# A new list of orders for block-sparse attention and an MLP on one core of a Trainium2

## The chip, the cores and the metric

The kernel runs on one core of one Trainium2 chip. Its engines work beside each other, each through its own instructions in order: PE (matrix products; PEld is its loading of weights), DVE, ACT and POOL (elementwise work), and SP, which here issues DMAs. The metric is the time of one execution on the device in microseconds (us), as the median of several. All operands of the large matrix products are 16-bit floats; sums are kept in 32 bits.

## The reference, cut to what matters

The inputs are q, k and v of shape (4, 8, 768, 64): batch, heads, positions, head dimension. Positions form 12 blocks of 64. Each position takes the 3 blocks with the highest gate score among those that are not later than its own, and its own block; it attends causally inside them. The result goes through a two-layer MLP with the tanh form of gelu.

```python
k_rep = k.reshape(B, H, 12, 64, D).mean(axis=3)
gate_scores = where(causal_block, einsum('bhsd,bhnd->bhsn', q, k_rep), -1e9)
top_idx = argsort(gate_scores, axis=-1)[..., -3:]
mask = (block in top_idx or own block) & (key position <= query position)
attn = softmax(where(mask, (q @ k.T) / 8, -1e9))
x = (attn @ v).transpose(0, 2, 1, 3).reshape(3072, 512)
out = gelu_tanh(x @ moe_w_in) @ moe_w_out          # 512 -> 2048 -> 512
```

## The kernel before, in words

**Tiling.** Heads are taken in pairs: pair p holds heads 2(p mod 4) and 2(p mod 4) + 1 of batch p // 4, so pairs 0 to 15. For each pair q, k and v are loaded, turned so that the head dimension lies on the partitions, and the block sums of k are formed. A gate product gives the block scores, DVE selects the top three, and the selection becomes a mask that is added to the scores. The scores are computed transposed, exponentiated by ACT, their diagonal edges are zeroed by POOL, and they are multiplied with v, which has a column of ones so that the row sums come with the product. The normed result is turned once more into xT. When four pairs of a batch are done, its 768 tokens go through the MLP: the first layer in 16 tiles of 128 hidden channels for two halves of 384 tokens (s1), the second per tile of 128 tokens (s2). In the last three batches some products are formed by seven half-size ones out of sums and differences on DVE (s1_seven, w_sums, half, join); this isn't touched.

**Buffers.** PSUM holds two wide buffers (scores and s1) and four banks, which pre, pv, ops, the tail and the fillers share by fixed numbers. Exponentials have six buffers (ats), the results two (osb, each for a pair of token tiles, so a new tile waits for the stores of the pair before the last), raw v two (vsd); k, q, v and the mask sets have four.

**What sets the order.** The kernel first adds 1962 numbered operations to a plan, each with the engines that can do it, and then emits them by three written lists: ORDER gives the sequence, and with it the order on each engine and in each queue; ENGINE sends some copies to ACT or POOL that else go to the first engine that the operation names (mostly DVE); BUFFER gives, in the order in which buffers are taken, which one. Waits between engines follow from the data and the buffers and are put in by the framework. An engine takes its instructions strictly in order, so one that waits holds all behind it.

```python
for n in ORDER:
    op = self.ops[n]
    for kind, key in op.takes:
        if key not in self.buf:
            self.buf[key] = self.kinds[kind][0][next(picks)]
    op.emit(engine.get(n, next(iter(op.engines))))
```

**Names and lines that the steps touch.** Loads: L387 (q, k, v as they lie), L393 (the ones that DVE turns), L421 (the first pair), cast of v to 16 bits in cast_v (L432, copies at L356 on ACT, L358 on POOL, L360 on DVE). The weights: load_w, a small copy (L451) that orders them behind the loads of v and two DMAs for each matrix issued by POOL (L453). Constants on POOL: the gates' constants (op 0, L480 to L484), the matrix e16 (op 1, a memset L491 and two affine selects L494), and four sets of memsets (ops 2, 3, 4, 5; L502 to L507). Pre, for each pair: transposes (L541) and, for k with block sums, L538; copies; the gate (L680) after the block sums (L582, L588); its turn to rows (L696); the selection sel_e: add the causal constant (L703), MAX8 (L712), compare (L713), and the mask value (L717); mask transposes on PE (L749) or by DMA (L756). Attention of batch 0 (heads2): scores L856, exponentials L875, edges on POOL L901, product with v L924, norm L942 and L943, turn L981. The others (heads): L1039, L1052, L1066, L1078. MLP: s1 L1115 with gelu L1127, s1_seven L1204, s2_plain L1315 with copies to osb and stores L1340, s2 L1365, L1414, L1449. The fillers are small products on zeros (L1517), numbered 1890 and up.

The single operations that the text speaks of: 62 and 71, the first half of k and of q of pair 0 turned on PE; 72 the copy of that q half; 73 and 74 the same for the second half of q; 75 the first gate and 77 its selection, 78 the second gate and 80 its selection; 105 the cast of q of pair 1 on POOL; 94, 114 and 130 copies of k; 30 the cast of v of pair 0 and 198 the first product with v; 139 and 141 the copies of q of pair 3, 142 its gate, 147 the copy of its mask; 227 a copy of turned results, 259 a norm; 363 the first s1 product; 157 and 163 the loads of w_in and w_out, 61 the cast of v of pair 3; 433 the first s2 product; 450, 468, 487, 505 the stores of token tiles 0, 1, 2, 3 of batch 0; 523 and 541 the copies to osb of tiles 4 and 5; 791 and 815 gelus of batch 1, 1044 a cast of q.

Of the kernel before, what the change touches and what calls it, by code (L numbers as in the profile page):

```python
# [21 lines left out]
    5, 2, 1890, 6, 1891, 1892, 1893, 9, 15, 0, 1894, 1895, 1896, 1897, 12,  # L22
    1898, 1899, 1900, 22, 1901, 1902, 1903, 23, 1904, 1905, 1906, 71, 72,
    62, 73, 195, 64, 63, 82, 75, 76, 66, 1907, 3, 77, 1908, 74, 1, 18, 1909,
    67, 1910, 100, 1911, 84, 68, 98, 85, 19, 35, 78, 4, 36, 83, 79, 80, 194,
    200, 99, 31, 89, 91, 101, 93, 86, 90, 120, 95, 87, 94, 196, 201, 121,
    32, 102, 219, 214, 202, 105, 220, 113, 103, 118, 215, 119, 1912, 26,
    109, 205, 104, 27, 197, 44, 115, 48, 106, 210, 107, 30, 198, 45, 111,
    110, 203, 221, 206, 234, 211, 122, 249, 207, 224, 123, 39, 208, 125,
    216, 235, 124, 133, 1913, 250, 240, 40, 229, 114, 251, 134, 212, 129,  # L30
    236, 126, 217, 135, 241, 222, 49, 43, 52, 245, 230, 225, 254, 242, 127,
    1914, 255, 238, 243, 138, 53, 140, 263, 246, 56, 57, 283, 58, 131, 247,
    130, 141, 1915, 1916, 139, 1917, 264, 252, 142, 231, 157, 284, 268, 279,
    256, 145, 232, 285, 143, 265, 269, 270, 1918, 226, 280, 274, 1919, 275,
    163, 144, 146, 276, 237, 61, 155, 227, 147, 288, 153, 1920, 259, 289,
    266, 297, 298, 302, 258, 271, 1921, 292, 272, 1922, 260, 299, 303, 1923,
    277, 149, 308, 322, 151, 323, 281, 286, 304, 169, 290, 293, 300, 309,
    305, 313, 317, 314, 310, 306, 170, 326, 261, 311, 294, 318, 328, 363,
    364, 295, 356, 315, 329, 365, 366, 358, 359, 319, 360, 361, 320, 324,
    327, 367, 362, 352, 353, 354, 355, 330, 171, 408, 174, 175, 357, 178,  # L40
    409, 410, 331, 411, 179, 412, 373, 374, 375, 376, 388, 389, 390, 391,
    377, 392, 403, 404, 405, 433, 393, 406, 434, 394, 395, 182, 396, 407,
    418, 419, 335, 420, 421, 397, 368, 369, 422, 370, 435, 398, 371, 399,
    436, 400, 372, 401, 383, 402, 384, 437, 385, 438, 439, 440, 441, 386,
    387, 336, 442, 443, 428, 429, 430, 444, 337, 183, 423, 186, 431, 424,
    432, 425, 339, 445, 341, 446, 447, 378, 448, 426, 379, 449, 427, 451,
    452, 453, 380, 187, 381, 345, 454, 631, 342, 343, 344, 334, 413, 414,
    632, 584, 692, 415, 346, 585, 455, 456, 457, 416, 458, 338, 635, 586,
    459, 417, 460, 461, 462, 636, 588, 347, 382, 463, 349, 553, 464, 465,
    466, 470, 348, 471, 574, 472, 570, 473, 474, 475, 571, 590, 476, 961,  # L50
    477, 572, 587, 575, 190, 478, 594, 479, 480, 481, 591, 482, 592, 483,
    593, 467, 566, 561, 484, 485, 644, 567, 488, 489, 552, 693, 596, 490,
    598, 491, 595, 562, 492, 493, 568, 557, 494, 569, 554, 647, 495, 645,
    597, 648, 555, 496, 558, 650, 497, 622, 486, 498, 563, 655, 601, 573,
    623, 499, 191, 651, 559, 618, 602, 500, 696, 654, 556, 652, 697, 619,
    576, 614, 653, 560, 624, 501, 577, 620, 502, 957, 578, 700, 503, 705,
    706, 609, 583, 958, 615, 709, 639, 656, 605, 504, 616, 507, 508, 610,
    509, 510, 564, 646, 511, 512, 513, 657, 617, 661, 621, 514, 640, 606,
    611, 962, 603, 515, 607, 665, 658, 625, 711, 662, 701, 666, 708, 1020,
    565, 712, 516, 669, 517, 678, 715, 604, 608, 713, 612, 714, 613, 670,  # L60
    1021, 679, 518, 671, 682, 1024, 707, 683, 717, 626, 519, 520, 521, 718,
    674, 522, 667, 716, 525, 468, 719, 526, 579, 663, 675, 643, 970, 726,
    680, 527, 676, 972, 684, 664, 668, 672, 735, 580, 1025, 727, 736, 528,
    728, 529, 730, 677, 450, 971, 673, 530, 722, 681, 731, 685, 739, 974,
    531, 704, 732, 723, 740, 532, 743, 627, 976, 724, 744, 533, 534, 1033,
    686, 725, 737, 628, 535, 544, 729, 981, 687, 1034, 745, 756, 733, 830,
    536, 741, 1082, 734, 738, 742, 746, 537, 1037, 523, 747, 538, 831, 539,
    758, 748, 977, 1039, 1040, 973, 1083, 749, 832, 833, 834, 759, 760, 761,
    540, 545, 768, 1035, 769, 770, 978, 1041, 1086, 771, 1036, 762, 979,
    752, 753, 548, 1144, 1145, 980, 1148, 1095, 772, 754, 965, 755, 763,  # L70
    1042, 764, 757, 765, 766, 840, 1096, 841, 767, 842, 1157, 1087, 1149,
    843, 844, 782, 773, 783, 784, 785, 546, 966, 792, 793, 786, 541, 982,
    1098, 774, 794, 795, 835, 1099, 1101, 836, 837, 838, 796, 1158, 825,
    839, 542, 775, 1163, 826, 1161, 827, 828, 811, 829, 1539, 1045, 549,
    812, 813, 1097, 1160, 814, 787, 1102, 1044, 1043, 1414, 845, 815, 1164,
    788, 789, 790, 806, 791, 984, 807, 808, 1410, 985, 809, 801, 802, 803,
    524, 810, 804, 777, 805, 778, 846, 779, 780, 781, 1165, 1415, 816, 817,
    818, 819, 820, 849, 1159, 1103, 1104, 847, 850, 851, 1166, 797, 852,
    821, 1002, 988, 853, 1047, 822, 798, 989, 969, 1477, 1003, 1004, 854,
    855, 856, 859, 860, 1048, 861, 862, 1540, 863, 997, 990, 991, 864, 998,  # L80
    1028, 857, 865, 858, 799, 993, 994, 1090, 866, 823, 992, 1478, 1006,
    1029, 547, 550, 1007, 868, 487, 869, 1010, 1008, 867, 870, 995, 871,
    1107, 1068, 872, 1005, 1009, 1011, 1064, 1069, 996, 1091, 1070, 1169,
    551, 999, 1065, 776, 873, 1072, 1012, 800, 874, 824, 875, 1051, 1094,
    1073, 877, 878, 848, 1059, 876, 1000, 1032, 1052, 879, 1013, 1105, 1014,
    1055, 1106, 1001, 880, 885, 505, 1411, 1110, 1066, 886, 1060, 887, 888,
    1074, 889, 890, 891, 1152, 1429, 892, 1067, 1071, 881, 1423, 1130, 1167,
    895, 1056, 896, 1057, 897, 1131, 1473, 898, 1474, 899, 1053, 900, 1075,
    901, 1126, 893, 1061, 1168, 1015, 902, 1425, 1127, 1109, 1128, 1597,
    1054, 1134, 894, 904, 1058, 1153, 882, 1113, 1135, 1535, 1062, 905,  # L90
    1554, 1172, 1114, 1117, 906, 1132, 1598, 907, 1171, 908, 1063, 1129,
    883, 1188, 903, 909, 1486, 910, 1118, 1119, 911, 1156, 1121, 1076, 913,
    1189, 912, 914, 915, 1492, 916, 1175, 1190, 921, 1122, 1543, 1115, 1487,
    1424, 1116, 922, 923, 1136, 1176, 924, 1544, 1120, 1123, 917, 1124, 925,
# [1525 lines left out]
```

## Time and profile before

| | |
|---|---|
| median of 3 runs | 253.68 us (253.64 to 253.81) |
| the profiled execution | 254.11 us |
| its span, first to last instruction | 252.4 us |
| granted TensorE clock | 1.00 |
| instructions in the profile | 6423 |
| first s1 product (op 363) | 38.24 us |
| last store issued | 249.29 us |

Times in the profile count from the start of the span. Rows of a timeline give start, duration, engine, line, operation, output and input, shape and count; the bracket at the end is the time that the engine sat idle before it, and whom it waited for. Busy times of PE are those of pipelined matmuls whose ends overlap, so the start of the next one says when PE was free. The span's 1.7 us of difference to the execution's own time lies outside what the profile shows.

### The profile page before, as it was taken

What the parts mean: (1) busy time and instruction counts of PE and PEld (TensorE: products, weight loads), DVE (VectorE), ACT (ScalarE), POOL (GpSimd) and SP (SyncE); (2) the same over time, 40 slices, a digit from 0 to 9 for tenths busy, and PEclk for the clock granted to TensorE, in tenths of its full rate; (3) what the DMA queues carried; (4) which work ended last, traced back from release to release, by engine and by line L of the source; (5) the groups of instructions that cost most, each with busy time, mean ns of one, the idle gap of its engine ahead of it and who ended that gap; (6) DMA issues with size and microseconds to landing.
All of it is one profiled execution on the core that took longest, in us unless ns stands there. A gap on an engine that the chain in (4) does not pass through costs nothing.

```text
span 252.4 us, 6423 instructions
## 1 busy us (share of the span) xinstructions
PE 244.2 (97%) x2483; PEld 170.4 (68%) x2483; DVE 188.6 (75%) x533; ACT 178.5 (71%) x225; POOL 86.8 (34%) x169
## 2 busy tenths in 40 slices
PE   7898999999999999999999999999999999999993
PEld 5665786555546666555778887656778887666883
DVE  2799863031869999999898977999775785687954
ACT  2577877546799999767899897757998927667300
POOL 8766860002135587240066644420244500000000
PEclk9999999999999999999999999999999999999999
DMA  8999599999999895999998996351601250020024
GB/s 153 219 207 184 88 211 180 214 151 160 141 153 130 155 198 93 146 176 181 167 204 145 223 154 114 88 118 42 166 4 24 41 180 20 3 84 0 4 92 158
DMA packets 130927, 32.62 MB, mean 129 GB/s; under 512 B 124528, under 2 KB 126928, under 8 KB 130896
## 3 DMA queue, kind: packets, MB, share of 16 engines
q1 hardware_dynamic: 126160, 27.62, 64.7%
q0 software_dynamic: 3136, 4.19, 10.0%
q10 hardware_dynamic: 1600, 0.39, 0.8%
q8 instruction: 19, 0.31, 0.6%
q14 instruction: 12, 0.10, 0.1%
HBM read 27.26 MB, written 6.29 MB: 133 GB/s over the span
## 4 chain that ended last, share of the span: by engine, by line
PE 91%; DVE 4%; DMA 2%; issue 1%; ACTq 1%; ACT 0%; DVEq 0%
PE wide L1115 27%; PE bank L1365 22%; PE wide L1039 11%; PE bank L1315 8%; PE bank L1078 6%; PE wide L1204 5%; PE wide L856 3%; PE bank L680 2%; PE bank L924 2%; DMA G<-in_q_dram 2%; PE bank L541 1%; PE bank L749 1%; PE bank L981 1%; DVE sel L712 1%; DVE sel L713 1%
## 5 line engine op out<-in xcount | busy, mean ns | idle before, releaser
L1115 PE MATMUL wide<-xT,w_in 128*128 128x384 f16 x416 | 74.1, 326 | 0.0
L1052 ACT ACTIVATE ats<-wide 128x896 f16<-128x896 f32 x72 | 62.0, 913 | 3.6 <-PE wide L1039 1.3
L1127 ACT ACTIVATE G<-wide 128x768 f16<-128x768 f32 x52 | 42.0, 809 | 27.0 <-PE wide L1115 25.3
L1115 PEld LDWEIGHTS <-w_in 128*128 128x128 f16 x416 | 39.9, 98 | 26.8 <-issue 1.3
L1066 POOL TENSOR_SCALAR_AFFINE_SELECT ats<-ats 128x256 f16<-128x256 f16 x72 | 31.3, 450 | 58.1 <-ACT ats L1052 57.8
L1039 PE MATMUL wide<-qT,kT 76*128 76x512 f16 (+3 forms) x192 | 38.6, 305 | 0.0
L557 DVE STREAM_TRANSPOSE s<-sd 128x768 f32<-128x768 f32 x24 | 23.2, 970 | 13.7 <-DMA sd<-in_k_dram 11.5
L1365 PE MATMUL bank<-w_out,G 128*128 128x256 f16 x216 | 31.9, 272 | 0.0
L1365 PEld LDWEIGHTS <-G 128*128 128x128 f16 x288 | 27.2, 98 | 5.2
L1315 PE MATMUL bank<-w_out,G 128*128 128x512 f16 x96 | 28.1, 379 | 0.0
L1414 DVE TENSOR_TENSOR osb<-bank,osb 128x512 f32<-128x512 f32 (+1 forms) x38 | 22.2, 594 | 7.0 <-PE bank L1365 6.5
L1039 PEld LDWEIGHTS <-kT 76*128 76x128 f16 x192 | 17.3, 97 | 10.6 <-issue 0.5
L875 ACT ACTIVATE ats<-wide 128x1024 f16<-128x1024 f32 (+3 forms) x24 | 21.0, 916 | 4.7 <-PE wide L856 4.6
L1078 PEld LDWEIGHTS <-ats 128*128 128x128 f16 x504 | 21.8, 97 | 3.6 <-POOL ats L1066 0.2
L358 POOL CAST kT<-s 64x768 f16<-64x768 f32 x23 | 19.5, 846 | 14.0 <-DVE s L557 13.2
L1078 PE MATMUL bank<-v,ats 128*128 128x65 f16 x504 | 24.1, 194 | 0.0
L1365 PEld LDWEIGHTS <-XS 128*128 128x128 f16 x216 | 20.0, 97 | 4.8
L1365 PE MATMUL bank<-TS,XS 128*128 128x256 f16 x144 | 22.8, 272 | 0.0
L358 POOL CAST v<-vsd 128x768 f16<-128x768 f32 x13 | 10.7, 828 | 30.9 <-DMA vsd<-in_v_dram 22.2
L356 ACT CAST qT<-s 64x768 f16<-64x768 f32 x21 | 17.4, 827 | 0.3
L962 DVE TENSOR_TENSOR xn<-bank,zr 128x384 f16<-128x384 f32 x24 | 13.4, 558 | 0.8
L712 DVE MAX8 sel<-sel 128x8 f32<-128x12 f32 x160 | 13.3, 157 | 0.6
(118 smaller groups left out, 350.3 us busy)
## 6 DMA issues: line engine op xcount, KB each, us to landing
out_dram<-osb SPq DMA_DIRECT2D x23, 256.0 KB
vsd<-in_v_dram SPq DMA_DIRECT2D x26, 192.0 KB
sd<-in_k_dram SPq DMA_DIRECT2D x48, 96.0 KB
sd<-in_q_dram SPq DMA_DIRECT2D x48, 96.0 KB
w_in<-in_moe_w_in_dram POOLq DMA_DIRECT2D x2, 1024.0 KB, 11.3
w_out<-in_moe_w_out_dram POOLq DMA_DIRECT2D x2, 1024.0 KB, 18.5
G<-in_q_dram SPq DMA_DIRECT2D x4, 192.0 KB
G<-in_k_dram SPq DMA_DIRECT2D x4, 192.0 KB
```

Source lines behind the costliest of these rows:

```text
L358: nc.gpsimd.tensor_copy(out=out, in_=in_)
L557: nc.vector.transpose(out=T[key + "T32", p], in_=T[key, p].rearrange("p t j -> p (t j)"))
L875: nc.scalar.activation(out=T["at", u][:, :, 0:n], in_=plan.buf[("st",) + u].rearrange("p (h w) -> p h w", h=2)[:, :, 0:n], func=AF.Exp, bi ...
L1039: nc.tensor.matmul(st[:, x:e], kT16[i][h][0:76, s0:s0 + 128], qT16[i][h][0:76, s0 + (x - cb):s0 + (e - cb)], start=True, stop=True)
L1052: nc.scalar.activation(out=T["at", u][:, 0:n], in_=plan.buf[("st",) + u][:, 0:n], func=AF.Exp, bias=0.0, scale=SCALE)
L1066: nc.gpsimd.affine_select(out=dg, in_=dg, compare_op=ALU.is_ge, fill=0.0, base=0, pattern=[[0, 2], [1, 128]], channel_multiplier=-1)
L1078: nc.tensor.matmul(pvv[:, qc, 0:65], at[:, cb + (qc - jc) * 128: cb + (qc - jc + 1) * 128], v16[i][:, jc, h, :], start=(gi == 0 and jc == ...
L1115: nc.tensor.matmul(hps[:, 512 * e:512 * e + HALF], w_in16[:, ci, (2 * j + e) * 128: (2 * j + e + 1) * 128], T["xT", b][:, ci, HALF * h:HAL ...
L1127: nc.scalar.activation(out=G[:, :, h, j, :], in_=plan.buf["hps", b, j, h].rearrange("p (e w) -> p e w", e=2)[:, :, 0:HALF], func=AF.Gelu_a ...
L1315: nc.tensor.matmul(plan.buf["ops", b, ti], G[:, f % 2, 2 * ti // NC, f // 2, ti % (NC // 2) * 128:ti % (NC // 2) * 128 + 128], w_out16[:, ...
L1365: nc.tensor.matmul(dst[:, HD * h:HD * h + HD], FACT[m][0][:, j, t * 128:(t + 1) * 128], FACT[m][1][:, j, :], start=(clear and j == 0), sto ...
L1414: nc.vector.tensor_tensor(out=dst(), in0=src(), in1=other(), op=ALU.add)
```

## The change

Only the three lists differ; every function is the same, letter for letter. The order has 1663 entries instead of 1666: the same 1629 operations that do work, and 34 fillers instead of 37 (1924, 1925 and 1926 are gone). Before op 363 stand 33 fillers instead of 34. Most engines' sequences are permuted from the first entries on; the last three operations (1846, 1888, 1848: a sum and two stores) keep their order. On SP the loads up to op 27 keep their order. POOL's first operations are 0, 1, 2, 5, 3 instead of 5, 2, 0, 3, 1. Gate 75 stands ahead of 73 instead of behind it. Op 163 (w_out) stands behind 61 and the edges 299 and 304 instead of ahead of 61.

Eleven copies leave ACT for DVE (114, 345, 346, 349, 595, 719, 1167, 1496, 1497, 1558, 1559), six go from DVE to ACT (94, 130, 655, 1620, 1621, 1698), and three leave POOL for DVE (338, 1426, 1488). Counts by engine: PE 882 to 879, DVE 287 to 295, ACT 219 to 214, POOL 139 to 136, SP 139 both. BUFFER has 545 entries instead of 548. The stores of tiles 0 and 1 of batch 0 (450, 468) go from places 60 and 58 of SP's sequence to 88 and 89, those of tiles 2 and 3 (487, 505) from 86 and 90 to 73 and 67; copy 523 goes from place 94 of ACT's sequence to 105.

```diff
--- before.py
+++ after.py
 ORDER = [
-    5, 2, 1890, 6, 1891, 1892, 1893, 9, 15, 0, 1894, 1895, 1896, 1897, 12,
-    1898, 1899, 1900, 22, 1901, 1902, 1903, 23, 1904, 1905, 1906, 71, 72,
-    62, 73, 195, 64, 63, 82, 75, 76, 66, 1907, 3, 77, 1908, 74, 1, 18, 1909,
-    67, 1910, 100, 1911, 84, 68, 98, 85, 19, 35, 78, 4, 36, 83, 79, 80, 194,
-    200, 99, 31, 89, 91, 101, 93, 86, 90, 120, 95, 87, 94, 196, 201, 121,
-    32, 102, 219, 214, 202, 105, 220, 113, 103, 118, 215, 119, 1912, 26,
-    109, 205, 104, 27, 197, 44, 115, 48, 106, 210, 107, 30, 198, 45, 111,
-    110, 203, 221, 206, 234, 211, 122, 249, 207, 224, 123, 39, 208, 125,
-    216, 235, 124, 133, 1913, 250, 240, 40, 229, 114, 251, 134, 212, 129,
-    236, 126, 217, 135, 241, 222, 49, 43, 52, 245, 230, 225, 254, 242, 127,
-    1914, 255, 238, 243, 138, 53, 140, 263, 246, 56, 57, 283, 58, 131, 247,
-    130, 141, 1915, 1916, 139, 1917, 264, 252, 142, 231, 157, 284, 268, 279,
-    256, 145, 232, 285, 143, 265, 269, 270, 1918, 226, 280, 274, 1919, 275,
-    163, 144, 146, 276, 237, 61, 155, 227, 147, 288, 153, 1920, 259, 289,
-    266, 297, 298, 302, 258, 271, 1921, 292, 272, 1922, 260, 299, 303, 1923,
-    277, 149, 308, 322, 151, 323, 281, 286, 304, 169, 290, 293, 300, 309,
-    305, 313, 317, 314, 310, 306, 170, 326, 261, 311, 294, 318, 328, 363,
-    364, 295, 356, 315, 329, 365, 366, 358, 359, 319, 360, 361, 320, 324,
...
-    536, 741, 1082, 734, 738, 742, 746, 537, 1037, 523, 747, 538, 831, 539,
...
-    1029, 547, 550, 1007, 868, 487, 869, 1010, 1008, 867, 870, 995, 871,
...
+    0, 1890, 6, 9, 1891, 1892, 1893, 1894, 1895, 15, 12, 1896, 1897, 1898,
+    1899, 1900, 1901, 1902, 1903, 1904, 1905, 62, 71, 1, 64, 1906, 1907, 72,
+    2, 22, 1908, 1909, 75, 23, 66, 1910, 1911, 18, 63, 76, 73, 77, 195, 67,
+    74, 68, 1912, 82, 98, 99, 84, 85, 100, 83, 78, 200, 19, 5, 194, 93, 35,
+    3, 36, 101, 201, 31, 89, 79, 32, 80, 26, 27, 86, 95, 91, 87, 39, 118,
+    105, 40, 196, 94, 119, 102, 205, 219, 120, 90, 109, 103, 113, 206, 48,
+    202, 1913, 104, 214, 1914, 115, 121, 106, 220, 4, 107, 197, 1915, 125,
+    1916, 111, 1917, 30, 210, 110, 215, 207, 249, 198, 211, 1918, 203, 221,
+    208, 49, 114, 44, 122, 240, 224, 45, 52, 250, 234, 43, 53, 140, 138,
+    212, 241, 123, 57, 235, 58, 216, 251, 124, 217, 222, 242, 141, 225, 153,
+    229, 236, 230, 56, 245, 139, 126, 238, 243, 133, 127, 135, 129, 254,
+    246, 130, 149, 231, 283, 255, 247, 131, 157, 252, 284, 263, 134, 264,
+    142, 274, 232, 256, 279, 275, 276, 143, 265, 145, 144, 259, 237, 280,
+    1919, 285, 268, 1920, 146, 269, 288, 147, 226, 266, 289, 270, 297, 298,
+    302, 1921, 61, 271, 292, 258, 227, 272, 277, 281, 286, 303, 308, 322,
+    323, 299, 290, 260, 304, 300, 163, 155, 1922, 293, 305, 317, 309, 313,
+    326, 151, 294, 318, 310, 328, 306, 363, 261, 314, 319, 356, 364, 295,
+    365, 169, 329, 366, 358, 311, 315, 359, 320, 170, 360, 324, 367, 361,
...
+    1095, 752, 753, 754, 772, 505, 755, 546, 763, 764, 765, 978, 757, 1041,
...
+    1163, 1161, 789, 790, 774, 487, 845, 806, 1164, 1102, 1159, 807, 846,
+    982, 808, 985, 1165, 809, 523, 791, 1103, 801, 1044, 1029, 524, 802,
+    803, 541, 804, 810, 777, 778, 779, 805, 1410, 1166, 780, 816, 1168,
...
+    878, 1065, 1073, 1059, 1009, 879, 450, 1055, 880, 885, 886, 1074, 1012,
...
 BUFFER = [
-    0, 1, 2, 3, 0, 1, 2, 3, 0, 1, 2, 3, 0, 1, 2, 3, 0, 1, 0, 2, 3, 0, 0, 1,
...
+    0, 1, 2, 3, 0, 1, 2, 3, 0, 1, 2, 3, 0, 1, 2, 3, 0, 1, 2, 3, 0, 2, 3, 1,
...
 ENGINE = {
     "ACT": [
-        63, 67, 74, 99, 101, 114, 119, 121, 345, 346, 349, 449, 467, 486,
-        504, 523, 541, 594, 595, 628, 654, 657, 715, 716, 719, 749, 893,
-        980, 981, 1043, 1044, 1105, 1106, 1167, 1168, 1202, 1433, 1434,
-        1496, 1497, 1558, 1559, 1668, 1674, 1677, 1704, 1707, 1727, 1733,
-        1736, 1786, 1822],
+        63, 67, 74, 94, 99, 101, 119, 121, 130, 449, 467, 486, 504, 523,
+        541, 594, 628, 654, 655, 657, 715, 716, 749, 893, 980, 981, 1043,
+        1044, 1105, 1106, 1168, 1202, 1433, 1434, 1620, 1621, 1668, 1674,
+        1677, 1698, 1704, 1707, 1727, 1733, 1736, 1786, 1822],
     "POOL": [
-        338, 586, 587, 646, 647, 707, 708, 972, 973, 1035, 1036, 1097, 1098,
-        1159, 1160, 1425, 1426, 1488, 1489, 1550, 1551, 1612, 1613]}
+        586, 587, 646, 647, 707, 708, 972, 973, 1035, 1036, 1097, 1098,
+        1159, 1160, 1425, 1489, 1550, 1551, 1612, 1613]}
```

257 rows, old and new, of tables (BUFFER, ORDER) are left out of this document.

## The prediction

> **What bounds the kernel now.** I read the profile's first part (busy time), then the windows by stage, then the chain of waits, and last the timelines of single engines around the places where the chain leaves the tensor engine. First the page's first part; then the windows: stage, its length, busy time of PE, PEld, DVE, ACT, POOL, clock, DMA share, GB/s. The four stages are the start, the opening up to the first matmul of the MLP's first layer (op 363, L1115), the body, and what follows the last matmul.
>
> ```profile
> PE 244.2 (97%) x2483; PEld 170.4 (68%) x2483; DVE 188.6 (75%) x533; ACT 178.5 (71%) x225; POOL 86.8 (34%) x169
> ...
> 0.00:4.80 4.80, 3.73 (x18) 2.43 (x18) 1.01 (x15) 1.49 (x2) 3.80 (x19) 1.00 0.66 133
> 4.80:38.24 33.44, 30.25 (x502) 23.19 (x502) 27.19 (x104) 23.67 (x32) 22.76 (x43) 1.00 1.06 184
> 38.24:248.50 210.26, 210.13 (x1969) 144.76 (x1966) 159.72 (x413) 153.33 (x192) 60.20 (x108) 1.00 0.72 120
> 248.50:252.40 3.90, 0.11 (x2) 0.00 (x0) 0.69 (x1) 0.00 (x0) 0.00 (x0) 1.00 0.46 168
> ```
>
> The body has 210.13 us of PE work in 210.26 us: no order of the same matmuls can shorten it by more than the 0.13 that is left and the fillers in it. The same windows for the filler line alone (PE and PEld columns):
>
> ```profile
> 4.80:38.24 33.44, 3.82 (x18) 1.59 (x17) 1.00 1.06 184
> 38.24:248.50 210.26, 0.71 (x3) 0.29 (x3) 1.00 0.72 120
> ```
>
> So the opening holds 30.25 - 3.82 = 26.4 us of real PE work in 33.44 us: about 7.0 us are fillers and waits. The tail's sum and store (ops 1846, 1848) stand last in both orders, behind the same matmuls; I put its change at 0. **The opening is where a new order can gain, and the body is where it can lose.**
>
> **Part one: the first selection.** Rows of PE, then DVE, then POOL (start, duration, what, and in brackets the idle time before):
>
> ```profile
> 6.74 0.52 PE L541 MATMUL bank<-identk,G 128*128 128x128 f32 x3 [0.76 <-DMA G<-in_q_dram]
> 7.19 0.32 PE L680 MATMUL bank<-s,ksb 128*32 128x64 f32 x8
> 9.99 0.29 PE L749 MATMUL bank<-ident,madd 128*128 128x128 f16 x2 [0.74 <-DVE madd L717]
> ...
> 5.35 0.56 DVE L360 COPY s<-bank 128x384 f32<-128x384 f32 x1 [3.05 <-PE bank L541]
> 7.93 0.71 DVE L703 TENSOR_TENSOR sel<-sel,cgate 128x48 f32<-128x48 f32 x1
> 9.11 0.51 DVE L713 TENSOR_TENSOR sel<-sel,sel 128x48 f32<-128x48 f32 x1
> 9.73 0.21 DVE L717 SCALAR_TENSOR_TENSOR madd<-sel,ownm 128x48 f16<-128x48 f32 x1
> 11.30 0.23 DVE L703 TENSOR_TENSOR sel<-sel,cgate 128x72 f32<-128x72 f32 x1
> 12.14 0.23 DVE L713 TENSOR_TENSOR sel<-sel,sel 128x72 f32<-128x72 f32 x1
> ...
> 7.69 1.87 POOL L494 TENSOR_SCALAR_AFFINE_SELECT G<-G 64x768 f16<-64x768 f16 x2
> 9.66 0.65 POOL L503 MEMSET madd<- 128x640 f16 x1
> 13.42 0.82 POOL L358 CAST XS<-s 128x768 f16<-128x768 f32 x1
> ```
>
> Before, gate 75 (7.19) stands behind the transposes of the second half of q (op 73), which wait for their DMA until 6.74; the q copy that the gate reads is ready at 5.35 + 0.56 = 5.91. After puts 75 ahead of 73, so it can go by 6.74 at the latest: 7.19 - 6.74 = **0.45 earlier**. The gate's matmuls then delay 73 by at most their 0.32, which no early reader needs.
>
> The selection behind it is slow for its size: 0.71 for 48 elements where 72 take 0.23 at 11.30, and 0.51 where 72 take 0.23 at 12.14. Both slow ones lie beside POOL's affine selects (7.69 to 9.56, op 1); L717 at 9.73 lies beside a MEMSET and takes only 0.21. After gives op 1 second place on POOL, behind op 0, ahead of the sets of memsets 2, 5 and 3 instead of behind them, so it is done before the first gate is: (0.71 - 0.23) + (0.51 - 0.23) = **0.76 earlier**. Together the first mask (9.99) comes about 1.2 earlier.
>
> But POOL's cast 105 (the 0.82 at 13.42) moves up, and would now lie beside the second selection. If it slows that one as the affine selects slowed the first, 0.28 (one instruction) to 0.76 (both) go back, and 0.45 to 0.9 are left. The Trainium skill, "SBUF — State Buffer", section "Who interferes with whom", says that a DVE instruction with two SBUF inputs contends with a GpSimd one that reads SBUF and not with one that only writes it, and that the loser blocks fully. The slow and fast rows above agree with it; by it the cast could cost its whole 0.82, and 0.4 would be left.
>
> **Part two: from there to the MLP.** The early gain cannot simply be carried on, since the first values land when they land:
>
> ```profile
> 16.83 0.83 POOL L358 CAST v<-G 128x768 f16<-128x768 f32 x1 [2.00 <-DMA G<-in_v_dram]
> ...
> 6.36 0.48 ACT L356 CAST XS<-bank 128x384 f16<-128x384 f32 x1 [1.86 <-DVE ksbx L588]
> ...
> 26.23 0.54 DVE L360 CAST XS<-bank 128x384 f16<-128x384 f32 x1
> 26.69 1.01 DVE L360 COPY s<-bank 128x384 f32<-128x384 f32 x2
> 28.53 0.35 DVE L696 STREAM_TRANSPOSE sel<-bank 128x160 f32<-128x160 f32 x1 [0.83 <-PE bank L680]
> 31.11 0.55 DVE L360 COPY xT<-bank 128x768 f16<-128x768 f16 x1
> 31.74 0.49 DVE L360 COPY XS<-bank 128x640 f16<-128x640 f16 x1
> ...
> 27.99 0.48 PE L680 MATMUL bank<-s,ksb 128*32 128x160 f32 x8
> ```
>
> POOL sat idle 2.00 us for v of pair 0, and SP's order up to that load is unchanged, so the first p.v (op 198) cannot start before 17.7 in either order. What After does is to place more scores ahead of 198 on PE, so the early gain is kept as work done and not as time past the landing; I count about half of it.
>
> Then the last selection of the opening (pair 3, 28.53). Its gate 142 waits for two q copies that end at 27.70. Cast 130 (0.54 at 26.23) leaves DVE for ACT, where such a cast takes 0.48, and runs later; the q copies move up by 26.69 - 26.23 = 0.46, and more by the 0.83 that DVE stood idle for the gate: 0.46 to 1.3 earlier. Cast 94 leaves DVE and 114 comes to it, which cancels. Mask copy 147 (31.74) is no longer behind copy 227 (0.55) but behind the norm 259, two DVE ops; I take this as even. Sum at op 363, which ran at 38.24: from 0.46, if nothing of part one gets past the landing, to 0.45 + 1.3 = 1.8. **I take 0.7**, nearer to the low end, since the 0.46 has a row of its own and of part one's 0.45 to 0.9 about half is to get through.
>
> A landing caps it:
>
> ```profile
> 26.63 1.66 POOL L453 DMA_DIRECT2D w_in<-in_moe_w_in_dram  x2 [0.35 <-issue]
> 30.70 1.78 POOL L453 DMA_DIRECT2D w_out<-in_moe_w_out_dram  x2
> ...
> DMA to landing us min/median/max: 9.1/11.3/13.5
> ...
> DMA to landing us min/median/max: 16.1/18.5/21.0
> ...
> 47.75 0.38 PE L1315 MATMUL bank<-w_out,G 128*128 128x512 f16 x1
> ```
>
> The two answers on landings are w_in's, then w_out's. The halves land at 26.63 + 9.1 = 35.7, 27.5 + 13.5 = 41.0, 30.70 + 16.1 = 46.8 and 31.6 + 21.0 = 52.6, so 5.3, 5.7 and 5.8 apart, one behind the other. The first matmul that reads w_out ran at 47.75, with as much PE work before it in both orders. 47.75 - 46.8 = 0.95: a larger gain than that is given back there, in part.
>
> **Part three: the body.** Fillers in it go from 3 to 1 by the order's places; the row above gives 0.71 / 3 = 0.24 each at most, and fillers that fill a wait are worth nothing: between 0 and -0.48, I take -0.2. The other moved steps (eleven copies from ACT to DVE, six to ACT, three from POOL to DVE, stores and loads in another order) lie beside PE work. Their cover, the PE work between a score matmul and what reads its exponentials, is as thin in the new order as in the old, at the smallest near zero. If a copy comes later than that, PE waits for the difference. Bounds: -0.13, all the idle time that the body has, and the price of the output copy below; I take +0.2, nearest to what the body shows now.
>
> **Sum.** Opening -0.7, fillers -0.2, body +0.2, tail 0: **-0.7**. The profiled execution took 254.11, of it 252.4 span and 1.71 around it; 254.11 - 0.7 = 253.4. It stood 0.43 above the median of 253.68, so for the median I forecast **253.0**. About 0.2%, or 0.5 us, is what a measurement of this kernel can tell from no change.
>
> **The rivals.**
>
> *The collisions are moved and the landing resets the rest: no change.* Cast 105 blocks the second selection for its whole 0.82, v's landing eats the 0.4 that remains of part one, and gate 142 comes 0.46 earlier but 0.2 of it are lost to the norm ahead of copy 147. Opening -0.3, fillers -0.1, body +0.3: 253.6. (The full 0.82 is what the Trainium skill's "SBUF — State Buffer" would make of it.) For it: the idle 2.00 at 16.83. Against it: the 0.83 at 28.53, which lies behind that landing.
>
> *An output copy holds ACT: slower.* Rows of ACT, then of SP's queue:
>
> ```profile
> 99.67 0.57 ACT L356 COPY osb<-bank 128x512 f32<-128x512 f32 x1
> 112.14 0.81 ACT L1127 ACTIVATE G<-wide 128x768 f16<-128x768 f32 x1 [0.49 <-PE wide L1115]
> 115.85 0.80 ACT L1127 ACTIVATE G<-wide 128x768 f16<-128x768 f32 x1
> ...
> 111.17 0.52 SPq L1340 DMA_DIRECT2D out_dram<-osb  x1
> 124.46 1.97 SPq L1340 DMA_DIRECT2D out_dram<-osb  x1
> 249.29 0.33 SPq L1449 DMA_DIRECT2D out_dram<-osb  x1
> ```
>
> Copy 523 (99.67) moves behind gelu 815 (115.85), and the buffer it writes is freed by stores 505 and 487, now at places 67 and 73 of SP's queue; place 73 was issued at 111.17. A store needs 0.33 to 1.97 to issue, and the last store needed 252.4 - 249.29 = 3.1 to the end of the span. 111.2 + 2.0 + 3.1 = 116.3 against 116.65 for the copy's turn: just in time, if nothing ahead of it on SP waits, and the first load of k for pair 13, which stood behind 487 before, now stands ahead of it. Behind the copy on ACT stand gelu 791, cast 1044 and more; PE, which fills two wide buffers ahead of the gelus, stalls for the delay D less the 0.49 that ACT has to spare in each unit. It decides from D of about 1.7 on (1.7 - 0.5 = 1.2 lost against 0.7 gained is 0.5 slower). For D = 3: 2.5 - 0.7 = +1.8, so 255.5.
>
> *w_out comes later: slower.* After issues w_out on POOL behind the cast of v of pair 3 and two edge ops of pair 3, four to five us later. If its 16.1 us counted from the issue, it would land some four us after the matmul at 47.75 wants it: 253.0 + 4 = 257. Against it: the even spacing of the four landings, by which w_out only waits behind w_in until 41.0, so that an issue five us later is still early.
>
> *The gain is larger*: the gate's chain gains 1.2 and 1.3 in full and the cap gives nothing back: 254.11 - 0.43 - 1.8 = 251.9.
>
> **How the numbers follow.** Forecast 0.46, larger gain 0.06, no change 0.20, output copy 0.23, w_out 0.05. Faster by over 0.5 us: 0.52; within: 0.20; slower: 0.28. The forecast's own range is 252.4 to 253.2. The range for 8 in 10 takes in no change and the output copy: 251.9 to 255.5; outside it lie w_out's case and the far ends of the larger gain and of a longer D.
>
> **What would show it.** Right: the first L703 and L713 near 0.23; the first gate below 6.8; pair 3's gate before 27.6; the first L1115 at 37.2 to 37.8; the first L1315 at 46.8 or later, without an idle time of more than 0.2 ahead of it; then one PE window without waits as before. Wrong: a second L703 or L713 above 0.5 and a first L1115 at 38 (no change); idle time of ACT ahead of an osb copy at 115 to 120 with PE waiting on L1115's wide buffer (slower); idle time of PE ahead of the first L1315 (w_out). The prediction falls if PE shows waits of more than 1 us in the body at any other place.

## The result, and the profile after

The changed kernel took 252.3 us (median of 11 runs, 251.47 to 253.61) beside 253.81 for the kernel before (median of 11, 252.82 to 254.47). The ratio is 0.9947 (95% interval 0.9926 to 0.9969): 1.3 us faster, by the interval between 0.8 and 1.9. Forecast were 253.0 us and a gain of 0.7; 252.3 lies 0.1 below the forecast's own range and inside the wide one, and nearer to the 251.9 of the larger gain than to the forecast. The profiled execution took 251.91 us with a span of 250.2. Line numbers are one smaller in after than in before, and five smaller in the kernels of the experiments (after_again has after's); the text goes by those of before where it names no row.

The stages of after, cut at the same events as those of before (first transposes, first s1 product, last product):

```profile
0.00:4.40 4.40, 3.33 (x16) 2.37 (x17) 0.92 (x15) 0.00 (x0) 3.55 (x13) 1.00 0.61 132
4.40:35.85 31.45, 30.16 (x494) 23.03 (x493) 25.21 (x104) 25.20 (x35) 22.65 (x49) 1.00 1.04 182
35.85:246.30 210.45, 210.36 (x1976) 144.79 (x1972) 161.50 (x422) 149.51 (x186) 58.99 (x105) 1.00 0.72 122
246.30:250.20 3.90, 0.00 (x1) 0.00 (x0) 0.69 (x1) 0.00 (x0) 0.00 (x0) 1.00 0.42 154
```

The body and the tail are as long as before (210.45 and 3.90), though the body's window now holds 7 more matmuls. The opening has shrunk from 33.44 to 31.45 us, and it starts 0.4 earlier: the gain lies there, and it is three times the 0.7 that was forecast for it. The chain of waits shows what stands in its way (shares of the span, by engine): first that of before, then that of after, by engine and by line.

```profile
PE 91%; DVE 4%; DMA 2%; issue 1%; ACTq 1%; ACT 0%; DVEq 0%
```
```profile
PE 80%; DMA 8%; SPq 6%; POOL 3%; issue 1%; DVE 0%; POOLq 0%
PE wide L1114 24%; PE bank L1364 22%; PE wide L1038 11%; PE bank L1314 9%; PE bank L1077 6%; SPq L386 6%; PE wide L1203 6%; DMA w_out<-in_moe_w_out_dram 5%; DMA TS<-in_v_dram 2%; PE bank L679 2%; POOL ats L900 2%; DMA G<-in_q_dram 1%; PE bank L980 1%; POOL v L357 1%; POOL w_in L452 1%
```

DVE has gone from 4% of the chain to 0%. In its place the chain runs through the loading of w_out, and from there back over POOL's issue to the loads of v. A share of the chain says who came last and not what could be won: ahead of the first product with w_out PE lost 0.26 us, as told below.

Where in the opening did it come from? Rows of PE in after, then DVE, then POOL:

```profile
6.35 0.32 PE L679 MATMUL bank<-s,ksb 128*32 128x64 f32 x8 [0.21 <-DVE s L359]
8.93 0.28 PE L748 MATMUL bank<-ident,madd 128*128 128x128 f16 x2
12.27 0.34 PE L748 MATMUL bank<-ident,madd 128*128 128x128 f16 x3 [0.26 <-DVE madd L716]
16.39 0.45 PE L748 MATMUL bank<-ident,madd 128*128 128x128 f16 x5 [0.24 <-DVE madd L716]
18.05 0.42 PE L923 MATMUL bank<-v,ats 128*128 128x65 f16 x8
18.89 0.48 PE L679 MATMUL bank<-s,ksb 128*32 128x160 f32 x8
22.61 0.45 PE L748 MATMUL bank<-ident,madd 128*128 128x128 f16 x5
25.91 0.48 PE L679 MATMUL bank<-s,ksb 128*32 128x160 f32 x8
46.01 0.38 PE L1314 MATMUL bank<-w_out,G 128*128 128x512 f16 x1
```
```profile
7.09 0.21 DVE L702 TENSOR_TENSOR sel<-sel,cgate 128x48 f32<-128x48 f32 x1
7.76 0.21 DVE L712 TENSOR_TENSOR sel<-sel,sel 128x48 f32<-128x48 f32 x1
10.23 0.88 DVE L702 TENSOR_TENSOR sel<-sel,cgate 128x72 f32<-128x72 f32 x1
15.44 0.89 DVE L716 SCALAR_TENSOR_TENSOR madd<-sel,ownm 128x120 f16<-128x120 f32 x1
16.83 0.20 DVE L581 TENSOR_TENSOR ksb<-bmask,ks 128x12 f32<-128x12 f32 x1
17.94 0.17 DVE L581 TENSOR_TENSOR ksb<-bmask,ks 128x12 f32<-128x12 f32 x1
21.20 0.36 DVE L712 TENSOR_TENSOR sel<-sel,sel 128x120 f32<-128x120 f32 x1
21.67 0.28 DVE L716 SCALAR_TENSOR_TENSOR madd<-sel,ownm 128x120 f16<-128x120 f32 x1
```
```profile
3.54 1.87 POOL L493 TENSOR_SCALAR_AFFINE_SELECT G<-G 64x768 f16<-64x768 f16 x2
10.20 0.82 POOL L357 CAST XS<-s 128x768 f16<-128x768 f32 x1 [0.85 <-ACT s L355]
15.37 0.82 POOL L357 CAST XS<-s 128x768 f16<-128x768 f32 x1 [2.11 <-ACT s L355]
16.14 0.89 POOL L357 CAST v<-G 128x768 f16<-128x768 f32 x1
```

And rows of before around pair 2's selection, which the prediction did not look at: PE, DVE, POOL.

```profile
19.23 0.48 PE L680 MATMUL bank<-s,ksb 128*32 128x160 f32 x8 [0.49 <-DVE ksb L582]
23.44 0.45 PE L749 MATMUL bank<-ident,madd 128*128 128x128 f16 x5 [0.80 <-DVE madd L717]
...
17.04 0.65 DVE L582 TENSOR_TENSOR ksb<-bmask,ks 128x12 f32<-128x12 f32 x1
18.58 0.60 DVE L582 TENSOR_TENSOR ksb<-bmask,ks 128x12 f32<-128x12 f32 x1
21.81 0.75 DVE L713 TENSOR_TENSOR sel<-sel,sel 128x120 f32<-128x120 f32 x1
22.66 0.72 DVE L717 SCALAR_TENSOR_TENSOR madd<-sel,ownm 128x120 f16<-128x120 f32 x1
...
18.33 0.82 POOL L358 CAST XS<-s 128x768 f16<-128x768 f32 x1
21.42 1.00 POOL L901 TENSOR_SCALAR_AFFINE_SELECT ats<-ats 128x256 f16<-128x256 f16 x2 [1.91 <-ACT ats L875]
22.37 0.87 POOL L358 CAST v<-TS 128x768 f16<-128x768 f32 x1
```

In before, PE waited 0.49 for pair 2's gate and 0.80 for its mask. The four DVE instructions ahead of these (two of L582, then L713 and L717) took 0.65, 0.60, 0.75 and 0.72, each beside a cast or an edge on POOL. In after the same four take 0.20, 0.17, 0.36 and 0.28, and PE waits for neither gate nor mask. In exchange two others are slow: 0.88 at 10.23 and 0.89 at 15.44, again beside POOL's casts, which start at 10.20 and 15.37. PE waits for the two masks behind them, 0.26 at 12.27 and 0.24 at 16.39.

To see where a lead is won and lost, I put the two traces side by side at equal PE work: the start times of all matmuls, each counted with the median pitch of its kind and the fillers with nothing. The lead over before's trace (negative is ahead, in us) is after 3 us of work (behind the first mask), 10 (first products with v, at about 18 us of time), 14 (behind pair 2's mask), 26 (the first s1 product), 38 (behind the first s2 product) and 230 (the end). The kernels below before and after are those of the experiments.

| kernel | 3 | 10 | 14 | 26 | 38 | 230 | ratio to before (95%) |
|---|---|---|---|---|---|---|---|
| after | -1.08 | -0.29 | -1.95 | -2.14 | -1.74 | -2.20 | 0.9947 (0.9926 to 0.9969) |
| after_again | -1.32 | -0.54 | -2.20 | -2.38 | -2.27 | -2.72 | 0.9930 (0.9911 to 0.9949) |
| open_new_body_old | -1.17 | -0.39 | -2.05 | -2.24 | -1.46 | -1.47 | 0.9993 (0.9976 to 1.0010) |
| splice_new_old | -0.74 | +0.05 | -1.62 | -1.81 | -1.78 | -1.78 | 0.9949 (0.9933 to 0.9965) |
| open_old_body_new | -0.21 | -0.17 | -0.16 | -0.14 | +0.75 | +1.08 | 1.0042 (1.0026 to 1.0058) |
| splice_old_new | -0.23 | -0.31 | -0.31 | -0.33 | -0.33 | -0.78 | 0.9991 (0.9980 to 1.0001) |
| before_new_pool | -0.79 | -0.24 | -1.51 | +0.14 | +0.42 | +0.41 | 1.0057 (1.0035 to 1.0080) |
| after_old_pool | -0.22 | +0.13 | -1.54 | -0.26 | -0.26 | -0.72 | 1.0003 (0.9991 to 1.0015) |
| first_selection_only | -0.62 | -0.23 | -1.54 | -1.70 | -1.49 | -1.51 | 0.9969 (0.9959 to 0.9979) |
| pair2_cast_later | -0.23 | -0.39 | -0.82 | -0.52 | -0.52 | -0.53 | 0.9992 (0.9983 to 1.0001) |
| w_out_use_late | -1.17 | -0.38 | -2.04 | -2.23 | -2.15 | -2.59 | 0.9934 (0.9913 to 0.9955) |
| w_late_memsets_first | -1.07 | -0.34 | -2.00 | -2.47 | -2.38 | -2.83 | 0.9906 (0.9891 to 0.9922) |
| q_cast_behind_v | -1.15 | -0.86 | -2.34 | -2.46 | -2.15 | -2.54 | 0.9899 (0.9884 to 0.9915) |

A row is one profiled execution against one of before, the ratio is many runs. The profiles of after, open_new_body_old and first_selection_only lie at the fast end of their runs and that of before at 254.11 some 0.3 us over its median, so a row's end is 0.7 to 1.3 us better than its ratio in these three; the columns are for finding the place. The two kernels with the old opening stand 0.14 and 0.33 ahead at 26: so much of every row there is the difference between executions and not the change.

After's row reads: 1.08 ahead at the first mask, 0.29 at the first products with v, 1.95 behind pair 2's mask, then almost level; 0.4 given back up to the first s2 products, 0.26 of it at w_out; 0.46 won in the body.

### The profile page after: what moved, and what is told of

It reads as the page before. It is cut to its first block, busy times and chain, and to the rows that moved or that the text cites. A ratio compares the mean times of both kernels' runs of the same rounds, so it can differ in the third digit from the quotient of the medians.

```text
span 250.2 us, 6424 instructions
## 1 busy us (share of the span) xinstructions
PE 243.9 (97%) x2480; PEld 170.2 (68%) x2480; DVE 188.3 (75%) x541; ACT 174.7 (70%) x220; POOL 85.2 (34%) x166
## 4 chain that ended last, share of the span: by engine, by line
PE 80%; DMA 8%; SPq 6%; POOL 3%; issue 1%; DVE 0%; POOLq 0%
PE wide L1114 24%; PE bank L1364 22%; PE wide L1038 11%; PE bank L1314 9%; PE bank L1077 6%; SPq L386 6%; PE wide L1203 6%; DMA w_out<-in_moe_w_out_dram 5%; DMA TS<-in_v_dram 2%; PE bank L679 2%; POOL ats L900 2%; DMA G<-in_q_dram 1%; PE bank L980 1%; POOL v L357 1%; POOL w_in L452 1%
## 5 line engine op out<-in xcount | busy, mean ns | idle before, releaser
L1065 POOL TENSOR_SCALAR_AFFINE_SELECT ats<-ats 128x256 f16<-128x256 f16 x72 | 32.0, 460 | 58.1 <-ACT ats L1051 57.7
L1364 PE MATMUL bank<-w_out,G 128*128 128x256 f16 x216 | 32.9, 272 | 0.0
L1314 PE MATMUL bank<-w_out,G 128*128 128x512 f16 x96 | 28.8, 379 | 0.1
L1077 PEld LDWEIGHTS <-ats 128*128 128x128 f16 x504 | 22.4, 98 | 3.8 <-POOL ats L1065 0.2
L357 POOL CAST kT<-s 64x768 f16<-64x768 f32 x20 | 17.1, 867 | 16.5 <-DVE s L556 16.1
L355 ACT CAST qT<-s 64x768 f16<-64x768 f32 x16 | 13.2, 828 | 0.2
```

The costliest lines, as they stand in the source:

```text
L357: nc.gpsimd.tensor_copy(out=out, in_=in_)
L1065: nc.gpsimd.affine_select(out=dg, in_=dg, compare_op=ALU.is_ge, fill=0.0, base=0, pattern=[[0, 2], [1, 128]], channel_multiplier=-1)
L1077: nc.tensor.matmul(pvv[:, qc, 0:65], at[:, cb + (qc - jc) * 128: cb + (qc - jc + 1) * 128], v16[i][:, jc, h, :], start=(gi == 0 and jc == ...
L1314: nc.tensor.matmul(plan.buf["ops", b, ti], G[:, f % 2, 2 * ti // NC, f // 2, ti % (NC // 2) * 128:ti % (NC // 2) * 128 + 128], w_out16[:, ...
L1364: nc.tensor.matmul(dst[:, HD * h:HD * h + HD], FACT[m][0][:, j, t * 128:(t + 1) * 128], FACT[m][1][:, j, :], start=(clear and j == 0), sto ...
```

## The experiments

**Is it the opening?** Two splices: the operations of the opening in one order, all others in the other.

```diff
-    ORDER = one list
+    ORDER = [n for n in new if n in opening] + [n for n in old if n not in opening]
```

> The operations of the opening (the 215 that stand ahead of the first s1 product in either order) in the new order, with the new buffers and engines; all others as before. Theory, the gain is made in the opening and carried through: at the first s1 product about 2.1 us earlier than before at equal PE work, of which the landing of w_out takes back about 0.3; total -1.6 to -2.0 us against before, ratio about 0.993. Rival, the old body doesn't fit the new opening and gives the gain back in waits: total within 0.5 us of before, with PE waits of 1 us or more after 46 us.

> The reverse: opening as before, all others in the new order. Theory: the body is worth only its fewer fillers and its few small waits, -0.2 to -0.5 us against before. Rival: the new body itself gains or loses more than 0.8 us.

Measured: ratios 0.9993 and 1.0042; by the totals the theory falls twice. The traces show why. In the first the lead is 2.24 at the first s1 product as in after, and 0.78 of it go at 39.95; in the second 0.89 go at 43.63. PE rows of either (the bracket has the idle time, the loss is counted from start to start):

```profile
39.95 1.46 PE L1110 MATMUL wide<-xT,w_in 128*128 128x384 f16 x8 [0.58 <-ACT G L1122]
```
```profile
43.63 5.04 PE L1110 MATMUL wide<-xT,w_in 128*128 128x384 f16 x30 [0.73 <-ACT G L1122]
```

Both are waits of s1 for a gelu, at the seam. Where the lists met, a wide buffer was taken twice in a row, so that PE had to wait for the gelu it should have run ahead of: a fault of my splices. With the wide buffers of the body exchanged they alternate there again, and no other buffer had to change:

```diff
-    BUFFER = picks of either list
+    BUFFER = the same, with wide 0 and wide 1 exchanged behind the opening
```

> The new opening with the old body, as in the first splice, but with the two wide buffers of the old body exchanged, so that they alternate across the seam (the first splice used one of them twice in a row, and PE waited 0.75 us there for a gelu). Theory, the gain is made in the opening: the trace is 2.1 us ahead of before at the first s1 product and stays 1.7 to 2.1 us ahead to the end; median -1.3 to -2.0 us. Rival, the old body gives it back: PE waits of over 0.5 us behind the seam.

> The old opening with the new body, mended in the same way (the first splice waited 0.90 us at the seam). Theory: -0.1 to -0.5 us from two fewer fillers and the small waits. Rival: a loss of over 0.5 us in the new body at a place where the mended seam has no part (the first splice had PE wait 0.95 us for a gate at 167.8).

Measured: 0.9949 for the new opening and 0.9991 for the new body, and their sum, -0.6%, is that of the whole change (-0.5% and, measured again below, -0.7%). The theory stands for the opening: about 1.3 us are its own. For the body the trace shows 0.45, but by many runs (0.9980 to 1.0001) its gain is not told apart from none. The second loss of the unmended splice, 0.95 us at a gate at 167.8, is not in the mended one; what it was stays open.

**POOL's order alone, and all but POOL's.** Only the sequence of POOL in the opening is exchanged, the other engines' sequences and all buffers stay:

```diff
-    POOL: 5, 2, 0, 3, 1, 4, 202, 105, 197, 30, 221, 207, 125, 216, 251, 236, 43, 242, 56, ...
+    POOL: 0, 1, 2, 5, 3, 105, 202, 4, 197, 125, 30, 207, 221, 43, 216, 251, 242, 236, 56, ...
```

> Before, with only POOL's own sequence in the opening taken from the new order (constants first, casts and edges permuted, w_out issued behind the cast of v of pair 3); every other engine's sequence, all buffers and engines as before. Theory C, collisions: DVE's slow two-input instructions of the opening beside POOL's work (L703 0.71, L713 0.51, L582 0.65 and 0.60, L713 0.75, L717 0.72) are what PE waited for, so POOL's order alone gives 0.7 to 1.5 us at the first s1 product, and these six become 0.2 to 0.4. Rival O, cover: the new order on PE and DVE puts work between each gate and its mask, and POOL's order alone gives less than 0.4 us or nothing.

> After, with only POOL's sequence in the opening as before. Theory C: the selections are slow again and the first s1 product comes 1 to 1.7 us later than in after, total about 253.3 to 254. Rival O: less than 0.4 us later than after, about 252.5.

Measured: 1.0057 and 1.0003, so neither half gives the gain. The table tells it by places. At 14 us of work each half alone is 1.5 ahead and both together 1.95. In before_new_pool five of the six slow instructions fall to between 0.21 and 0.28, as expected, and one stays at 0.64. In after_old_pool those of the first selection are slow again (0.55 and 0.51), but pair 2's four are not. For pair 2 the traces tell collisions from cover. Its four instructions take 2.6 to 2.8 us together in the three kernels with before's opening, and PE waits 0.49 for the gate and 0.80 for the mask; they take 1.43 in before_new_pool, 1.27 in after_old_pool and 1.01 in after, and PE waits for neither. before_new_pool has before's own order on PE, so no new cover was needed for that. Behind pair 2, each half loses it all again. PE rows of before_new_pool, then of after_old_pool:

```profile
31.76 0.42 PE L919 MATMUL bank<-v,ats 128*128 128x65 f16 x8 [1.28 <-POOL ats L896]
32.52 0.28 PE L851 MATMUL wide<-XS,XS 64*128 64x256 f16 x2 [0.34 <-POOL XS L353]
```
```profile
23.90 0.60 PE L919 MATMUL bank<-v,ats 128*128 128x65 f16 x12 [0.41 <-POOL v L353]
33.73 0.74 PE L919 MATMUL bank<-v,ats 128*128 128x65 f16 x18 [0.90 <-POOL ats L896]
```

PE, in its order, waits for an edge or a cast that POOL, in the other order, does later: 1.28 and 0.34 in one, 0.41 and 0.90 in the other. The edge that the last row waits for starts at 33.25 on POOL, as the issue of w_out ends that stands ahead of it (31.47, 1.78 us); after has that issue behind this edge. Theory C is right up to pair 2's mask, and wrong that the order of POOL alone would bring a gain at the end. Of after_old_pool it forecast the total (253.61), but only the first selection lost it in the way that it names. Rival O is right that POOL's order alone gives nothing at the end, but not for its reason; and after_old_pool is 1.9 behind after at the first s1 product where it allowed 0.4.

**The two steps that the prediction priced, alone.**

```diff
-    5, 2, ... 0, ... 62, 73, 195, 64, 63, 82, 75, 76, ... 74, 1, 18,
+    0, 1, 5, 2, ... 62, 195, 64, 63, 82, 75, 73, 76, ... 74, 18,
```

> Before, with only the first two steps of the prediction: POOL does ops 0 and 1 ahead of its memsets (order 0, 1, 5, 2, 3), and the first gate (op 75) stands ahead of the second half of q (op 73). Theory now, the landing of v takes the early lead back unless later operations fill it: 0.7 to 1.2 us ahead of before at the first mask, at most 0.3 us behind the first product with v, median 0 to -0.3 us. Rival, the lead is carried: half or more of it is there at the first s1 product, median -0.5 us or better.

Measured: 0.9969, or -0.8 us, more than half of the whole change as first measured and less than half as measured again. My theory fell, though the lead does shrink to 0.23 at the first products with v as it said. But it shrinks by another way: L717 of pair 1's selection starts beside the cast of v (15.53) and takes 0.86 for 0.28, and PE waits 0.59 for that mask, not for v. The first step doesn't show in this execution: the gate runs at 7.21 (7.19 in before), since the first products were slow (the last section tells of this), and the lead at the first mask is 0.62 where 0.7 to 1.2 were expected. The lead grows again to 1.54 four us later. DVE rows:

```profile
16.98 0.17 DVE L577 TENSOR_TENSOR ksb<-bmask,ks 128x12 f32<-128x12 f32 x1
18.09 0.20 DVE L577 TENSOR_TENSOR ksb<-bmask,ks 128x12 f32<-128x12 f32 x1
20.92 0.28 DVE L708 TENSOR_TENSOR sel<-sel,sel 128x120 f32<-128x120 f32 x1
21.31 0.53 DVE L712 SCALAR_TENSOR_TENSOR madd<-sel,ownm 128x120 f16<-128x120 f32 x1
```

No step of pair 2 was touched, and three of its four slow instructions are fast, the fourth takes 0.53 for 0.72. POOL is ahead of DVE here: v of pair 0 is cast at 15.53 instead of 16.83 and is done when L582 starts at 16.98 (17.04 in before), so DVE meets POOL's work elsewhere. POOL waited for v's landing in both, and v landed earlier here with the same loads ahead of it; why, and whether it does so in most runs, is not shown. The rival's condition, half or more at the first s1 product, is met (1.70 ahead), but the early lead was not carried: it was won anew.

**One collision alone.** The cast of v of pair 1 goes one place down on POOL:

```diff
-    POOL: ... 236, 43, 242, 56
+    POOL: ... 236, 242, 43, 56
```

> Before, with a single POOL operation moved: the cast of v of pair 1 (op 43) one place later, behind the edge op 242, so that it no longer starts beside L717 of pair 2's selection (0.72 us there, 0.28 elsewhere). Theory, the collision is what the mask of pair 2 waits for: L717 takes 0.28, the mask comes about 0.4 us earlier, PE's wait ahead of it goes from 0.80 to about 0.4, and 0.2 to 0.4 us are left at the first s1 product. Rival: the mask comes no earlier, or products with v wait for the later cast and nothing is left.

Measured in the trace (DVE, then PE):

```profile
22.28 0.28 DVE L712 SCALAR_TENSOR_TENSOR madd<-sel,ownm 128x120 f16<-128x120 f32 x1
...
22.62 0.45 PE L744 MATMUL bank<-ident,madd 128*128 128x128 f16 x5 [0.37 <-DVE madd L712]
```

L717 takes 0.28 for 0.72 and PE waits 0.37 for 0.80: 0.43 won by moving one cast, as the theory said (the lead grows from 0.39 to 0.82). Of it 0.30 are lost at pair 3, where L703 now takes 0.68. The ratio, 0.9992, is not told apart from no change.

**The changed kernel again, and w_out.** In the second kernel the first s2 product stands where the second one does:

```diff
-    337, 433, 407, 393, 391, 394, 434,
+    337, 407, 393, 391, 394, 433, 434,
```

> The changed kernel once more, beside the others on one chip. Theory: ratio 0.993 to 0.997 again; a second trace with the same lead at the first s1 product within 0.4 us. If its runs spread over 2 us again, the second trace tells by its landings which part of that the opening makes.

> After, with the first s2 product (op 433) moved three s1 products later on PE, to where the second one stands (about 1.1 us). Theory, w_out's landing caps the opening's gain: the wait of 0.26 us at 46.0 goes, and the lead over before grows from 1.74 to 2.0 us at 50 us; median 0.2 to 0.3 us below after. Rival: the wait isn't w_out's, or comes back at the next s2 product; no change against after.

Measured: 0.9930 and 0.9934; of the first, what was expected holds (2.38 ahead at the first s1 product, 2.14 in the first trace). In after PE lost 0.26, counted from start to start, ahead of its first s2 product, and w_out's first half had landed at 33.54 + 12.4 = 45.9 by these rows:

```profile
26.67 1.66 POOL L452 DMA_DIRECT2D w_in<-in_moe_w_in_dram  x2 [0.18 <-issue]
33.54 1.78 POOL L452 DMA_DIRECT2D w_out<-in_moe_w_out_dram  x2
...
DMA to landing us min/median/max: 8.3/10.8/13.2
...
DMA to landing us min/median/max: 12.4/14.9/17.4
```

In after_again the loss there is 0.11, and with the product moved it is gone. So the wait is w_out's, it is small, and moving its reader brings nothing that the medians show (251.76 and 251.71); the 0.2 to 0.3 us that were expected against after are not there.

**A better version.** Two more moves on POOL, for the two slow instructions that after has: set 3's memsets (op 4) ahead of cast 105, and, in the second kernel, cast 125 behind the cast of v of pair 0 and its edges.

```diff
-    POOL: 0, 1, 2, 5, 3, 105, 202, 4, 197, 125, 30, 207, 221, ...
+    POOL: 0, 1, 2, 5, 3, 4, 105, 202, 197, 30, 207, 221, 125, ...
```

> After, with the first s2 product later as in the run before, and with the memsets of set 3 (op 4) ahead of the cast of q of pair 1 (op 105) on POOL, so that L703 of the second selection (0.88 us in after) starts beside memsets. Theory: L703 falls to about 0.25, the second mask comes 0.3 to 0.6 us earlier and its wait of 0.26 goes; the landing of v takes most of it back; median 0 to -0.3 us against after. Rival: the cast now meets L713 or pair 1's scores wait for it; no gain or a loss of up to 0.4.

> The run above, and also the cast of q of pair 2 (op 125) behind the cast of v of pair 0 and its two edges, so that L717 of pair 1's selection (0.89 us in after, beside that cast) starts alone. Theory: L717 falls to 0.28, the mask of pair 1 comes 0.5 us earlier and its wait of 0.24 us goes, but the block sums behind it (L582) now meet the casts and lose 0.4 each; 0 to -0.4 us against the run above. Rival: the sums lose as much as the mask gains and pair 2's gate comes no earlier.

Measured: 0.9906 and 0.9899, medians 251.43 and 251.40 (4 runs each) where before took 253.78. Both beat before. By the median both beat after and its repetition too, but the intervals overlap that of after_again, so that is not shown. In the first, L703 falls from 0.88 to 0.23, but a cast on DVE from SBUF to SBUF now lies beside the memsets and L713 beside cast 105, where it takes 0.47 for 0.23:

```profile
9.45 0.84 DVE L355 CAST XS<-s 128x384 f16<-128x384 f32 x1
...
10.51 0.23 DVE L698 TENSOR_TENSOR sel<-sel,cgate 128x72 f32<-128x72 f32 x1
```

So the second mask comes no earlier (its product runs at 12.22, in after at 12.27) and the theory's step fails. In the second kernel L717 falls to 0.28, the product of pair 1's mask runs at 15.82 instead of 16.34 without a wait, and the lead at 10 us of work is 0.86 instead of 0.34; the block sums behind it take 0.45 and 0.60, as was expected. Pair 2's gate comes 0.32 earlier, against the rival. At the end the two kernels are equal, so none of this is left that the medians show.

## Why the prediction was right or wrong

**What bounds the kernel: right.** The body has kept its length, the gain is the opening's, the tail didn't move.

**Part one: right, with luck in the parts.** L703 and L713 of the first selection take 0.21 each (0.23 forecast), the gate stands at 6.35 (6.74 at the latest forecast), and the product of the first mask at 8.93 instead of 9.99: 1.06 for the 1.2 worked out. The mask itself was ready at 8.29 instead of 9.94; its product then stood behind another transpose on PE, which waited for its q until 8.58. And the gate's time hangs on the execution: with the same opening it stood at 7.26 in splice_new_old. The moved cast 105 does slow the second selection, by 0.88 - 0.23 = 0.65, inside the bounds of 0.28 and 0.76. The Trainium skill, "SBUF — State Buffer", section "Who interferes with whom", says that a DVE instruction with two SBUF inputs contends with a GpSimd one that reads SBUF; these rows agree with that. So the change moves collisions, as the prediction said.

**Half of it past the landing of v: right in size by luck, wrong in the reason.** The lead did fall from 1.08 to 0.29 at the first products with v, but after's trace shows no wait for v: its cast ends at 17.03, and the first product with v starts a microsecond later, at 18.05, without idle time. Between the first mask and that product PE waits 0.26 and 0.24 for the two masks that POOL's casts delayed, and runs five fillers of about 0.11 us where before has one. q_cast_behind_v takes one of the two collisions away, and 0.86 of the lead is left there instead of 0.34.

**The step that failed is part two's, "then the last selection of the opening (pair 3)".** From v's landing the prediction went straight to pair 3 and gave it 0.46 to 1.3. Pair 2's selection lies between them, with PE waits of 0.49 and 0.80 in before's trace and four DVE instructions that took 2.72 us together and 1.01 in after. There the lead grew by 1.66 us. That these instructions are the cause is shown for one of them by pair2_cast_later; for the others the traces agree, since every one that has them fast has no wait there. Pair 3's gate then came 2.08 earlier, but 1.95 of lead were there already behind pair 2's mask and 2.14 at the first s1 product: pair 3 itself brought about 0.2, and the 0.83 that DVE stood idle there was no reserve of its own. The sum at op 363 was forecast as 0.7, at most 1.8, and was 2.1 in this trace; by many runs the new opening gives 1.3. So the first s1 product and the first s2 product (35.85 and 46.01) miss the signs that were set for them (37.2 to 37.8, and 46.8 or later).

**The cap by w_out: mis-sized.** The prediction took the landing at 46.8 as fixed and 0.95 as all that could pass. It came at 45.9, with the first half of w_in at 35.0 instead of 35.7, so 1.74 passed. The landing moves from execution to execution: with before's order on POOL it lay between 45.6 (splice_old_new, pair2_cast_later) and 46.8 (before), so 0.95 was read from a late one. The prediction was right that it is a cap, and that the later issue does no harm: 33.54 instead of 30.70, and the landing was no later.

**The body: a little better than forecast, in the traces.** -0.2 for fillers and +0.2 for later stalls were set, together nothing. In the traces it gave 0.46 (after) and 0.45 (splice_old_new), and no new stall of note came; by many runs splice_old_new is not told apart from before.

**The rivals.** "No change" by moved collisions: the collisions moved, and the two new ones cost PE 0.26 and 0.24, but those of pair 2 went, which the rival left out as well. w_out did not land later, so that rival did not come true. The output copy that holds ACT did not happen: rows of ACT, then of SP,

```profile
113.40 0.58 ACT L355 COPY osb<-bank 128x512 f32<-128x512 f32 x1
...
102.23 1.86 SPq L1339 DMA_DIRECT2D out_dram<-osb  x1
108.32 0.77 SPq L1339 DMA_DIRECT2D out_dram<-osb  x1
```

the second store was issued 5 us ahead of the copy's turn, and the copy started without a wait.

## What to carry to other kernels

Where two engines slow each other, the path is not a list of durations: go through every instruction that is slower than its like (0.65 against 0.17, 0.72 against 0.28) and see what lies beside it, at each stage up to the end and not only at the first. A change of order ahead of it decides which instruction meets which, so a lead that is lost at one place can come back at the next, and a forecast that follows only the first collision misses it. And an order of one engine is worth something only with the others' orders: POOL's new order alone gave nothing, nor did all the rest without it.

## What the runs showed of the hardware

Which instructions meet: DVE's with two inputs in SBUF (L703, L713, L717, L582) take up to 0.65 us longer if a cast or an edge runs on POOL as they start (L703 0.88 for 0.23), and 0.28 as ever if it starts behind them (L717 at 20.93 in before_new_pool, a cast at 21.09); the norm (L943), with one input in PSUM, took 0.56 at every place in the opening, beside casts too, and memsets did nothing to any of these (L703 0.21 beside memsets in after). DVE's cast from SBUF to SBUF is another thing: 0.84 in the row at 9.45 above, where it started as POOL began a memset of 0.64 us, and 0.35 in after at 9.45, where POOL was idle.

The first products are not equally fast in each execution. The same six matmuls at the same place of the same opening, in after and in splice_new_old, with a granted clock of 1.00 in both:

```profile
4.46 0.92 PE L537 MATMUL bank<-identk,G 128*128 128x130 f32 x6
```
```profile
4.46 1.54 PE L533 MATMUL bank<-identk,G 128*128 128x130 f32 x6
```

The slow pitch, 0.22 us from start to start instead of 0.11, lasted until about 6.4 there, and the first gate came at 7.26 instead of 6.35. Of these 0.91 us no more than 0.33 are left at the first s1 product (1.81 ahead of before, and 2.14). The Trainium skill, "TensorE: Matmul & The Clock Gate", "Part 1: The HAM clock gate (the "warmup" mystery)", has the array slow until a free-running window has seen it busy, so that the moment differs from run to run, by ±500 ns. These rows agree with that in kind, though the granted clock of the profile doesn't show it; but the moment lay between 4.0 us (w_out_use_late) and 6.8 us (before_new_pool), with the first product at 1.07 in both, and the measured spread counts. How much of the 2 us between runs of one kernel comes from this is not shown.
